# Four edits around the output stage and the last weight gradients of a one-core forward and backward kernel: a later first load of w2 rows, whole-piece weight transposes, log-dt turned as bf16, another PSUM pool for the last output tile

## The chip, the core and the metric

The kernel runs on one core of a Trainium2 chip. Its engines are TensorE (PE in the profile; PEld is its weight load), VectorE (DVE), ScalarE (ACT), GpSimd (POOL) and SyncE (SP). Each works through its own instruction stream in order; an instruction waits for the semaphores of what it depends on, and everything behind it on the same engine waits too. SP, ACT and POOL also issue DMAs, which move data between device memory and the on-chip memories (SBUF, and PSUM, into which PE writes). "SPq" marks a DMA instruction on SP; its time is the time SP is held by issuing it, not the transfer. The metric is the device time of one execution, in microseconds.

## The reference, cut to what matters

The kernel computes a block's output and the gradients of all its parameters. `x` is 2048 tokens by D = 576, F is 4608.

```python
xn = layernorm(x)
s = ssm(xn, A, B, C, log_dt, Dskip)               # a long convolution, dt = exp(log_dt)
g = silu(((silu(xn @ w1) * (xn @ w3)) @ w2))      # SwiGLU, then silu
out = x + s * g
_out, vjp = jax.vjp(f, x, A_re, A_im, B_re, B_im, C_re, C_im, log_dt, Dskip, w1, w3, w2)
return (_out, *vjp(grad_out))
```

Three results of the backward half matter here: the gradients of w1, w3 and w2 (out_10 to out_12); the gradient of the input, which needs the two hidden gradients times the transposed w1 and w3 (out_1); and the gradients of the recurrence's parameters, which need dt (out_2 to out_8).

## The kernel before, in words

Tokens are cut into 16 tiles of 128, F into 36 blocks of 128 and, for the backward half, into 18 groups of 256. The order on each engine comes from a scheduler that takes instructions by a due time (`self.at`); `issue_after(x)` puts an instruction behind x, `sp`, `gp` and `sc` chain the instructions of one queue, and the pools decide which buffer a tile gets and what must have let go of it.

**Forward.** A hidden stage computes both gate products and stores h in device memory as `H_dram`, while the convolution runs beside it. The output stage (`ffn_output`) multiplies h by w2: for each token tile i, `begin(i)` turns the tile's 4608 columns of h onto the partitions by one transposing DMA on SP (`hcA`, `hcB` and `hcC` in turn; the DMA is kept in `hc_loads[i]`), and `product` runs 72 matmuls (`po`) into one of three PSUM pools, psA, psB, psC, chosen by i % 3. `finish(i)` then reads `po` with one ACT and two DVE instructions (lines 1119, 1122, 1123), forms out_0 and the gradient that goes into the SwiGLU (`go_o`), and PE turns that (`turn_go`, line 1165).

**Backward.** `backward` opens a pool of three one-bank PSUM tiles (`ph`) and one of two (`pgw`) in the space that psA, psB and psC leave. For each of the 18 groups it needs the group's w2 turned (`w2T`): two rows of blocks are loaded as `w2r` (line 1618) and turned by SP (`phase6_load_w2`, through the helper line 1640, `nat_transpose`). Line 1708 forms the hidden gradient `ph`, line 1726 (DVE) the two products `gu_n` and `gg_n`, line 1731 stores them (`GU_dram`, `GG_dram`), line 1748 makes w2's gradient and line 1768 those of w1 and w3. Between them run the backward convolution (lines 816 to 862, 1267 to 1329) and, from group 4 on, the parameter sums (`param_step`: `qT`, `gz` and `pz` are loaded by SP, line 1372 on PE, lines 1377 and 1380 on DVE).

**The turned weights.** The input gradient (`phase6_inputs`, line 1818, `px`) takes 72 blocks: for each token tile the rows of `GG_dram` and `GU_dram` are turned into `acts`, and multiplied with the rows of w1 and w3 turned. 15 blocks of w1 and 11 of w3 have room of their own (`wA`) and are loaded over earlier groups. The other 46 go into buffers as the groups free them, by `load_piece`: six pieces of 7 blocks and two of 2. One piece (`h_n` tag, blocks 22 to 28 of w3) is loaded in the last group but one, three at the stage "h1" of the last group, then come the group's stores, the `acts` of two tiles, and the last four pieces. A piece is loaded by five transposing DMAs, one for each 128 (the last 64) of the 576 rows. `ready` counts the blocks with which both first token tiles begin.

**log-dt.** `phase5_open` loads the 576 values as five rows (`lg_b`) on POOL in the last group's stage "h3", ACT takes the exponential (line 1398, `er_b`, fp32), and `phase5_turn` turns the result on PE (line 1404) and copies it from PSUM on DVE (line 1405). Both tiles rotate through the three `gh6` buffers.

```python
with self.tc.issue_after(self.hc_loads[4].ins):       # backward, line 1520
    self.w2row_load(0)
for c in range(self.cfg.DT):                          # load_piece, line 1624
    self.load_wT_rows(wT[-1], c)
self.nat_transpose(w2T[:, fl], self.w2rows[gi % 2][:, fl])   # phase6_load_w2, line 1652
```

Of the kernel before, what the change touches and what calls it, by code (L numbers as in the profile page):

```python
# [10 lines left out]
ACT = mybir.ActivationFunctionType  # L11
ALU = mybir.AluOpType
AX = mybir.AxisListType
FP32 = mybir.dt.float32
BF16 = mybir.dt.bfloat16
I32 = mybir.dt.int32
I16 = mybir.dt.int16
P = 128
# [68 lines left out]
class K:  # L87
# [24 lines left out]
    def pool(self, **kw):  # L112
        return self.tc.tile_pool(reuse_waits="tile", **kw)
# [928 lines left out]
    def ffn_output(self, T0, TB):  # L1042
        nc, cfg = self.nc, self.cfg
        D, DT, L, LT, F, FT = cfg.D, cfg.DT, cfg.L, cfg.LT, cfg.F, cfg.FT
# [7 lines left out]
        with self.pool(name="o_gap", bufs=1) as gap, \  # L1052
# [38 lines left out]
            def begin(i):  # L1091
                self.at(T0 + TB * i)
                hc = (self.wtp, hp, hpc)[i % 3].tile([P, FT, P], BF16, name="hc" + "ABC"[i % 3], tag=("WT", "hcB", "hcC")[i % 3])
                for f0, f1, step in turns[i] if i < 3 else ((0, FT, None),):
                    with self.tc.issue_after(self.h_stores[step].ins) if step else nullcontext():
                        ld = self.nat_transpose(hc[:, f0:f1], self.H_dram[i][:, f0 * P:f1 * P])
                self.hc_loads.append(ld)
                x_t = ip3.tile([P, D], BF16, name="x_t")
                go_t = ip3.tile([P, D], BF16, name="go_t")
                s_t = ip4.tile([P, D], BF16, name="s_t4")  # L1100
                nc.gpsimd.dma_start(out=x_t[:], in_=self.tok("A_u", i))
                nc.gpsimd.dma_start(out=go_t[:], in_=self.tok("grad_out", i))
                nc.gpsimd.dma_start(out=s_t[:], in_=self.S_dram[:, i, :])
                return i, hc, x_t, go_t, s_t, (psA, psB, psC)[i % 3].tile([P, 2, 512], FP32, name="po")

            def product(st, f0, f1, after=None):
                hc, po_ = st[1], st[5]
# [7 lines left out]
            def finish(st):  # L1115
# [23 lines left out]
                if i < LT - 1:  # L1139
                    self.turn_go(i, pst.tile([P, DT, P], BF16, name="ptr"))  # L1140

            first = begin(0)
            self.at(self.gate_time(70) - 1)
            product(first, 0, F0, self.tails[69])
# [10 lines left out]
            for i in range(2, LT):  # L1155
                st = begin(i)
                product(st, 0, FT)
                finish(st)
# [224 lines left out]
    def phase5_open(self, pool):  # L1383
        nc, cfg = self.nc, self.cfg
        self.fp = pool
        self.NB = -(-cfg.D // P)
        NB = self.NB
        lr = pool.tile([NB, P], BF16, name="lg_b", tag="gh6")
        st = self.small.tile([P, 3 * NB + 3], FP32, name="sm_b")
        self.dtb = st[:, 0:2 * NB].rearrange("p (k j) -> p k j", k=2)  # L1390
        self.gl = st[:, 2 * NB:3 * NB]
        self.acc = st[:, 3 * NB:]
        nc.vector.memset(lr[:], 0.0)
        nc.vector.memset(self.gl, 0.0)
        for row, vec in self.block_rows(lr, self.aps["A_log_dt"]):
            nc.gpsimd.dma_start(out=row, in_=vec)  # L1396
        self.er = er = pool.tile([NB, P], FP32, name="er_b", tag="gh6")
        nc.scalar.activation(out=er[:], in_=lr[:], func=ACT.Exp)

    def phase5_turn(self):  # L1400
        nc, NB, er = self.nc, self.NB, self.er
        pt = self.ps_T.tile([P, 512], FP32, name="et_ps")
        with self.tc.issue_after(self.pe_last.ins):
            nc.tensor.transpose(pt[:, 0:NB], er[:], self.ident_f[0:NB, 0:NB])
        nc.vector.tensor_copy(out=self.dtb[:, 0], in_=pt[:, 0:NB])
        nc.vector.tensor_tensor(out=self.dtb[:, 1], in0=self.dtb[:, 0], in1=self.dtb[:, 0], op=ALU.mult)
        self.final = self.phase5_blocks()
        self.final_rows = None
# [86 lines left out]
    def backward(self, T0, TG, TQ, TC, TX, gctx, mats):  # L1495
        nc, cfg = self.nc, self.cfg
        D, L, LT, F, FT = cfg.D, cfg.L, cfg.LT, cfg.F, cfg.FT
# [7 lines left out]
        pool = self.pool  # L1505
        PS = bass.MemoryType.PSUM
        FA, GP = 14, 11
        with ExitStack() as out:
# [4 lines left out]
            elp = out.enter_context(pool(name="e_el", bufs=3))  # L1513
# [3 lines left out]
            self.w2rows = [rowp.tile([P, self.FG // P, cfg.DT * P], BF16, name=f"w2r{i}") for i in range(2)]  # L1517
            for w2r in self.w2rows:
                nc.gpsimd.memset(w2r[:, :, D:cfg.DT * P], 0.0)
            with self.tc.issue_after(self.hc_loads[4].ins):  # L1520
                self.w2row_load(0)
            ps_h = ffn.enter_context(pool(name="e_ps_h", bufs=3, space=PS, side="right"))
            ps_gw = ffn.enter_context(pool(name="e_ps_gw", bufs=2, space=PS, side="right"))
# [22 lines left out]
            wT = []  # L1546
            for ai, n in ((0, 15), (1, 11)):
                wT.append((ai, 0, n, wA.tile([P, n, D], BF16, name=f"wA{ai}")))
            self.params_open(S_all, ps)
            step = self.param_step  # L1550
            hs = {}
            for gi in range(NG):
                self.chain = gi >= GP
                lastg = gi == NG - 1
                nxt = self.phase6_load(gi + 1, T0 + TG * gi, TG, wp, inp) if not lastg else None
                prep = nxt[-1] if nxt else iter(())
                if lastg:
                    self.tail()
                self.at(T0 + TG * gi)
                hs[gi] = cur[1]  # L1560
                w2 = lambda g, fl: self.phase6_grad2(g, fl, hs[g], gwp, ps_gw)
                for stage in group if gi == 0 else self.phase6_group(gi, cur, elp, gwp, ps_h, ps_gw):
                    if stage == "h3" and self.chain and gi + 2 < NG:
                        self.w2Ts[gi + 2] = self.phase6_load_w2(gi + 2, wp)
                    if stage in ("h2", "h3", "out_11_0", "out_11_1", "out_11_2", "out_11_3", "out_10_0", "out_10_1"):
                        next(prep, None)
                    if stage in ("h1", "h3"):
                        if gi < NG - 1:
                            w2(gi, stage == "h3")
                        elif stage == "h3":  # L1570
                            self.phase5_open(elp)
                        if stage == "h3" and gi + 2 < NG:
                            self.phase6_load_h(gi + 2, T0 + TG * gi, inp)
                    if stage == "out_11" and gi == NG - 2:
                        self.load_piece(wT, inp, "h_n", 1, 22, 7)
                    if stage == "h1" and lastg:
                        self.load_piece(wT, inp, "gg_n", 0, 15, 7)
                        self.load_piece(wT, inp, "gu_n", 1, 15, 7)
                        self.load_piece(wT, wp, "w2T", 1, 13, 2)
                    if stage == "end" and 0 <= gi - GP < cfg.DT:  # L1580
                        for part in wT[0:2]:
                            self.load_wT_rows(part, gi - GP)
                    if stage == "stored":
                        c = gi - GP
                        if c in (1, 2, 3, 4):
                            step()
                        if lastg:
                            self.hold = []
                            self.phase5_turn()
                            acts = [self.load_acts(0)]  # L1590
                            for fl in range(2):
                                w2(gi, fl)
                                step()
                                self.phase5_step(self.half // 2)
                                self.phase5_step(self.half // 2)
                            acts.append(self.load_acts(1))
                            self.ready = sum(part[2] for part in wT)
                            self.load_piece(wT, wp, "w2T", 1, 11, 2)
                            self.load_piece(wT, inp, "h_n", 0, 22, 7)
                    elif stage in ("h1", "h3", "out_11", "out_10", "end") and gi >= GP and not (lastg and stage in ("out_10", "end")):  # L1600
                        step()
                        if lastg and stage == "out_11":
                            self.phase5_step(self.half // 2)
                            self.phase5_step(self.half // 2)
                cur = nxt
# [15 lines left out]
    def load_piece(self, wT, pool, tag, ai, f0, n):  # L1621
        t = pool.tile([P, n, self.cfg.D], BF16, name=f"wT{ai}_{f0}", tag=tag)
        wT.append((ai, f0, n, t))
        for c in range(self.cfg.DT):
            self.load_wT_rows(wT[-1], c)

    def load_wT_rows(self, part, c):
        ai, f0, n, t = part
# [19 lines left out]
    def phase6_load_w2(self, gi, wp):  # L1648
        nfl = self.FG // P
        w2T = wp.tile([P, nfl, self.cfg.DT, P], BF16, name="w2T")  # L1650
        for fl in range(nfl):
            self.nat_transpose(w2T[:, fl], self.w2rows[gi % 2][:, fl])
        if (gi + 1) * self.FG < self.cfg.F:
            self.w2row_load(gi + 1)
        return w2T
# [341 lines left out]
```

## Time and profile before

| | us |
|---|---|
| three runs | 1818.41, 1829.12, 1833.62 |
| their median | 1829.12 |
| the profiled execution | 1822.4 |
| its span, first to last instruction | 1820.6 |
| PE busy | 1664.9 (91%) |
| VectorE busy | 1358.7 (75%) |
| ScalarE busy | 911.6 (50%) |
| mean granted TensorE clock | 0.982 |

Busy time says how long an engine had work in hand. What an edit is worth is read from the waits: a line of the waits such as `A <- B: 9.9, 5, 3.0` says that A waited 9.9 us in total for B, in 5 waits of at most 3.0 us. In a timeline a row gives start, time, engine, line, operation, tiles and count, and in brackets the idle time before it with what ended it. "DMA share" is the busy share of the 16 DMA engines.

| stretch of the profiled execution, us | what runs | PE busy | DMA share |
|---|---|---|---|
| 605 to 635 | output stage, tiles 5 to 7 | 22.93 of 30 | 1.16 |
| 635 to 704 | output stage, tiles 7 to 13 | 66.84 of 69 | 0.86 |
| 724 to 745 | end of the last output tile, group 0 opens | 16.91 of 21 | 0.76 |
| 745 to 765 | convolution and group 0 | 12.32 of 20 | 0.11 |
| 1436 to 1456 | last group | 14.46 of 20 | 0.82 |
| 1475 to 1490 | first input-gradient tiles | 12.68 of 15 | 1.14 |
| 1490 to 1505 | the same, last pieces being turned | 14.73 of 15 | 0.86 |
| 1505 to 1522 | the same | 7.82 of 17 | 0.94 |
| 1540 to 1560 | token tile 2 of the input gradient | 13.36 of 20 | 1.15 |

### The profile page before, as it was taken

What the parts mean: (1) busy time and instruction counts of PE and PEld (TensorE: products, weight loads), DVE (VectorE), ACT (ScalarE), POOL (GpSimd) and SP (SyncE); (2) the same over time, 40 slices, a digit from 0 to 9 for tenths busy, and PEclk for the clock granted to TensorE, in tenths of its full rate; (3) what the DMA queues carried; (4) which work ended last, traced back from release to release, by engine and by line L of the source; (5) the groups of instructions that cost most, each with busy time, mean ns of one, the idle gap of its engine ahead of it and who ended that gap; (6) DMA issues with size and microseconds to landing.
All of it is one profiled execution on the core that took longest, in us unless ns stands there. A gap on an engine that the chain in (4) does not pass through costs nothing. (4 is left out here: it accounts for less than half of the span.)

```text
span 1820.6 us, 38755 instructions
## 1 busy us (share of the span) xinstructions
PE 1664.9 (91%) x15573; PEld 1232.7 (68%) x15637; DVE 1358.7 (75%) x2103; ACT 911.6 (50%) x1648; POOL 346.3 (19%) x565
## 2 busy tenths in 40 slices
PE   7789999999999899799999999999899896999997
PEld 3455555554546677678888888888688774777885
DVE  7778888795873455767977879569899945878675
ACT  6778888776862111765756666554345310001001
POOL 3112222123143110011111101111111233131032
PEclk9999999999999999899999999999999998999999
DMA  7889998879699985478665756689999999999992
GB/s 221 275 280 344 321 343 312 279 266 285 208 296 226 222 208 150 149 217 237 188 192 174 208 162 203 165 253 241 253 228 226 195 225 207 236 217 224 220 251 52
DMA packets 636506, 416.91 MB, mean 229 GB/s; under 512 B 425430, under 2 KB 576966, under 8 KB 631718
## 3 DMA queue, kind: packets, MB, share of 16 engines
q1 hardware_dynamic: 580644, 287.34, 63.6%
q0 software_dynamic: 31904, 106.81, 18.2%
q10 hardware_dynamic: 23778, 20.28, 4.1%
q8 instruction: 122, 2.00, 0.5%
q14 instruction: 58, 0.48, 0.1%
HBM read 135.60 MB, written 190.89 MB: 179 GB/s over the span
## 5 line engine op out<-in xcount | busy, mean ns | idle before, releaser
L1818 PEld LDWEIGHTS <-acts 128*128 128x128 bf16 x2304 | 226.0, 99 | 81.5 <-DMA acts<-GU_dram 9.2
L1768 PEld LDWEIGHTS <-xn_bf 128*128 128x128 bf16 x2304 | 224.8, 98 | 46.7 <-issue 20.2
L1818 PE MATMUL px<-wT,acts 128*128 128x288 bf16 x1472 | 193.3, 289 | 9.9 <-DMA wT<-in_B_w_dram 9.9
L1377 DVE TENSOR_TENSOR pr_q<-et_ps,pz 128x1024 f32<-128x1024 f32 x144 | 175.8, 1221 | 27.0 <-PE et_ps L1372 10.5
L1708 PE MATMUL ph<-w2T,goT 128*128 128x256 bf16 x1440 | 175.5, 275 | 6.1 <-ACT gh L1711 3.4
L1011 PEld LDWEIGHTS <-xnT 128*128 128x128 bf16 x1152 | 107.0, 98 | 108.8 <-issue 17.7
L1380 DVE TENSOR_REDUCE S_all<-pr_q 128x32 f32<-128x1024 f32 x144 | 175.2, 1217 | 3.1
L1708 PEld LDWEIGHTS <-goT 128*128 128x128 bf16 x1440 | 140.4, 99 | 25.4 <-issue 5.4
L1011 PE MATMUL pu<-wmB_w,xnT 128*128 128x512 bf16 x568 | 152.9, 379 | 0.5 <-issue 0.2
L1748 PE MATMUL pgw<-go_o,h_n 128*128 128x288 bf16 x1152 | 150.0, 288 | 3.4 <-DVE h_n L1686 2.7
L1011 PE MATMUL pg<-wmB_w,xnT 128*128 128x512 bf16 x526 | 143.6, 379 | 8.2 <-issue 5.6
L1768 PE MATMUL pgw<-gu_n,xn_bf 128*128 128x256 bf16 x1152 | 136.6, 274 | 12.2 <-ACT gw L1752 6.2
L1748 PEld LDWEIGHTS <-h_n 128*128 128x128 bf16 x1152 | 113.1, 99 | 32.4 <-DVE h_n L1686 3.0
L1768 PE MATMUL pgw<-gg_n,xn_bf 128*128 128x256 bf16 x1152 | 130.4, 272 | 2.4 <-ACT gw L1770 2.3
L1770 ACT CAST gw<-pgw 128x256 bf16<-128x256 f32 x144 | 52.2, 373 | 147.3 <-PE pgw L1768 147.2
L1025 ACT ACTIVATE s_t<-pg 128x512 bf16<-128x512 f32 x144 | 87.8, 610 | 73.6 <-PE pu L1019 42.8
L1818 PE MATMUL px<-wA,acts 128*128 128x288 bf16 x832 | 112.0, 291 | 11.7 <-DMA acts<-GU_dram 8.6
L1711 ACT CAST gh<-ph 128x512 bf16<-128x512 f32 x144 | 80.9, 597 | 63.7 <-PE ph L1708 63.1
L660 ACT ACTIVATE cs_k<-et_ps 128x512 bf16<-128x512 int16 x216 | 111.5, 633 | 0.1
L1039 POOL DMA_DIRECT2D G_dram<-g_t x72 | 52.2, 726 | 288.1 <-DVE g_t L1029 146.2
L1874 ACT ACTIVATE go<-gx 128x576 bf16<-128x576 f32 x16 | 10.9, 683 | 188.8 <-DVE gx L1857 105.3
L1030 ACT CAST u_t<-pu 128x512 bf16<-128x512 f32 x144 | 87.5, 608 | 7.6 <-PE pu L1011 7.5
(317 smaller groups left out, 3208.9 us busy)
## 6 DMA issues: line engine op xcount, KB each, us to landing
U_dram<-u_t POOLq DMA_DIRECT2D x72, 256.0 KB, 5.6
G_dram<-g_t POOLq DMA_DIRECT2D x72, 256.0 KB, 5.0
H_dram<-h_t SPq DMA_DIRECT2D x72, 256.0 KB, 3.9
Q_dram<-q_k SPq DMA_DIRECT2D x36, 512.0 KB, 4.5
h_n<-U_dram POOLq DMA_DIRECT2D x18, 1024.0 KB, 8.8
gg_n<-G_dram POOLq DMA_DIRECT2D x18, 1024.0 KB, 6.7
GU_dram<-gu_n SPq DMA_DIRECT2D x36, 512.0 KB, 5.0
GG_dram<-gg_n SPq DMA_DIRECT2D x36, 512.0 KB, 10.3
```

The costliest lines, as they stand in the source:

```text
L660: self.sin_last = nc.scalar.activation(out=CS[:, :, o:o + 256], in_=pt[:].bitcast(I16)[:, :, 0::2], func=ACT.Sin, scale=6.283184 / 2 ** 16)
L1011: ins = nc.tensor.matmul(pt[:], lhsT=xnT[:, c, ts], rhs=wm[w][:, c, :], start=(q == 0 and c == 0), stop=(q == 1 and c == nfull - 1))
L1025: nc.scalar.activation(out=s_t[:, :, q, :], in_=pgv, func=ACT.Silu)
L1030: nc.scalar.copy(out=u_t[:, :, q, :], in_=puv)
L1039: self.u_stores[step] = nc.gpsimd.dma_start(out=dst[fb * ng:(fb + 1) * ng, :, i0:i0 + NT, :].rearrange("g p t f -> p g (t f)"), in_=src[:] ...
L1377: nc.vector.tensor_tensor(out=pr[:].rearrange("p r k e -> p r (k e)"), in0=T[h][:].rearrange("p k z d a -> p (k z d a)")[:, None].to_broad ...
L1380: nc.vector.tensor_reduce(out=self.S_all[:, :, d0:d0 + 4], in_=pr[:].rearrange("p r k (d a) -> p (r k) d a", d=4), op=ALU.add, axis=AX.X)
L1708: self.pe_last = nc.tensor.matmul(ph[j][:, k, :].rearrange("p (a f) -> p a f", f=P), lhsT=lw, rhs=rh, start=(n == 0), stop=(n == nfull))
L1711: self.sc(lambda: nc.scalar.copy(out=gh[:, j], in_=ph[j][:]))
L1748: self.pe_last = nc.tensor.matmul(pgw[pi_][:, 0:pw], lhsT=hn[:, tt, fl * P:(fl + 1) * P], rhs=go_o[:, tt, po:po + pw], start=(tt == 0), st ...
L1768: self.pe_last = nc.tensor.matmul(pw_[:, 0:FG], lhsT=self.xn_bf[:, tt, c * P:(c + 1) * P], rhs=nat[:, tt, :], start=(tt == 0), stop=(tt == ...
L1818: self.pe_last = nc.tensor.matmul(px[pi_][:, 0:pw], lhsT=acts[i][:, ai, fi, :], rhs=w[:, po:po + pw], start=(n == 0), stop=(n == len(steps ...
```

## The change

It makes four edits.

1. The last output tile takes PSUM pool psC, like the tile before it, instead of psA.
2. The first w2 rows (`w2row_load(0)`) are put behind the output stage's eighth tile load instead of the fifth, and group 0's turned w2 behind the fourteenth.
3. A weight piece is turned by one DMA of 576 source rows instead of five of 128 or 64. `wA` is still loaded in rows.
4. log-dt is loaded when the backward half opens, into a tile of its own (`lg_r`), on POOL's chained queue. PE turns it as bf16, and ACT takes the exponential from PSUM straight into `dtb`; the DVE copy goes.

```diff
@@ ffn_output, begin @@
-                return i, hc, x_t, go_t, s_t, (psA, psB, psC)[i % 3].tile([P, 2, 512], FP32, name="po")
+                return i, hc, x_t, go_t, s_t, (psA, psB, psC)[i % 3 if i < LT - 1 else 2].tile([P, 2, 512], FP32, name="po")
@@ phase5_open @@
-        lr = pool.tile([NB, P], BF16, name="lg_b", tag="gh6")
+        self.lr = lr = self.small.tile([NB, P], BF16, name="lg_r")
...
         for row, vec in self.block_rows(lr, self.aps["A_log_dt"]):
-            nc.gpsimd.dma_start(out=row, in_=vec)
-        self.er = er = pool.tile([NB, P], FP32, name="er_b", tag="gh6")
-        nc.scalar.activation(out=er[:], in_=lr[:], func=ACT.Exp)
+            self.gp(lambda: nc.gpsimd.dma_start(out=row, in_=vec))
@@ phase5_turn @@
-        pt = self.ps_T.tile([P, 512], FP32, name="et_ps")
+        pt = self.ps_T.tile([P, 512], FP32, name="et_ps")[:].bitcast(BF16)[:, 0:NB]
         with self.tc.issue_after(self.pe_last.ins):
-            nc.tensor.transpose(pt[:, 0:NB], er[:], self.ident_f[0:NB, 0:NB])
-        nc.vector.tensor_copy(out=self.dtb[:, 0], in_=pt[:, 0:NB])
+            nc.tensor.transpose(pt, self.lr[:], self.ident_bf[0:NB, 0:NB])
+        nc.scalar.activation(out=self.dtb[:, 0], in_=pt, func=ACT.Exp)
@@ backward @@
-            with self.tc.issue_after(self.hc_loads[4].ins):
+            with self.tc.issue_after(self.hc_loads[7].ins):
                 self.w2row_load(0)
...
             self.params_open(S_all, ps)
+            self.phase5_open(elp)
...
-                        elif stage == "h3":
-                            self.phase5_open(elp)
@@ load_piece @@
-        for c in range(self.cfg.DT):
-            self.load_wT_rows(wT[-1], c)
+        self.nat_transpose(t[:], self.aps[("B_w1", "B_w3")[ai]][:, f0 * P:(f0 + n) * P])
@@ phase6_load_w2 @@
         for fl in range(nfl):
-            self.nat_transpose(w2T[:, fl], self.w2rows[gi % 2][:, fl])
+            with self.tc.issue_after(self.hc_loads[13].ins) if gi == 0 else nullcontext():
+                self.nat_transpose(w2T[:, fl], self.w2rows[gi % 2][:, fl])
```

In the order of instructions that the scheduler makes of it, three things move beyond the edited lines. On SP, the four w2T transposes of groups 0 and 1 go from between the loads of tiles 4 and 6 to between those of tiles 13 and 14, and four of the six w2r loads that stood among them with them. On PE, 21 `ph` matmuls of group 0 stand ahead of the last output tile's first matmul. On DVE and ACT, the convolution's work after the last output tile is ordered anew: the `gk_st` evictions of lines 1322 and 1325 for the first two blocks stand ahead of group 0's Silu (line 1678) on ACT, and on DVE one fold (lines 1267, 1268) and a further part of the convolution's products (lines 856 to 862) stand ahead of group 0's lines 1685 and 1686.

More of the change, by code (lines that the diff above doesn't have):

```diff
@@ L1395, in phase5_open @@
         for row, vec in self.block_rows(lr, self.aps["A_log_dt"]):
-            nc.gpsimd.dma_start(out=row, in_=vec)
-        self.er = er = pool.tile([NB, P], FP32, name="er_b", tag="gh6")
-        nc.scalar.activation(out=er[:], in_=lr[:], func=ACT.Exp)
+            self.gp(lambda: nc.gpsimd.dma_start(out=row, in_=vec))
     def phase5_turn(self):
-        nc, NB, er = self.nc, self.NB, self.er
-        pt = self.ps_T.tile([P, 512], FP32, name="et_ps")
+        nc, NB = self.nc, self.NB
+        pt = self.ps_T.tile([P, 512], FP32, name="et_ps")[:].bitcast(BF16)[:, 0:NB]
         with self.tc.issue_after(self.pe_last.ins):
-            nc.tensor.transpose(pt[:, 0:NB], er[:], self.ident_f[0:NB, 0:NB])
-        nc.vector.tensor_copy(out=self.dtb[:, 0], in_=pt[:, 0:NB])
+            nc.tensor.transpose(pt, self.lr[:], self.ident_bf[0:NB, 0:NB])
+        nc.scalar.activation(out=self.dtb[:, 0], in_=pt, func=ACT.Exp)
         nc.vector.tensor_tensor(out=self.dtb[:, 1], in0=self.dtb[:, 0], in1=self.dtb[:, 0], op=ALU.mult)
```

## The prediction

> **What bounds the kernel now.** I read the chain of work that ended last, then PE's waits by stretch, then SP's timeline where a wait ends on a DMA.
>
> ```profile
> PE 14%; SPq 3%; DMA 2%; DVE 1%; issue 0%; ACT 0%; POOL 0%; ACTq 0%; DVEq 0%
> ```
>
> The chain is followed back through the last fifth of the span only, and PE has 14 of those 20 points: PE sets the end, and the rest is SP and its transfers. So an edit is worth what it takes from PE's waits. Those from the last group on (1400 to 1821), in us, times, longest:
>
> ```profile
> PE px L1818 <- DMA wT<-in_B_w_dram: 9.9, 5, 3.0
> PE px L1818 <- DMA acts<-GU_dram: 8.6, 2, 7.8
> PE et_ps L1372 <- DMA gz<-gK_dram: 7.1, 3, 3.6
> PE et_ps L1404 <- ACT er_b L1398: 4.4, 1, 4.4
> PE px L1818 <- DMA acts<-GG_dram: 3.1, 1, 3.1
> ```
>
> SP there, as start, time held, instruction:
>
> ```profile
> 1435.69 20.32 SPq L1640 DMA_TRANSPOSE wT<-in_B_w_dram  x15
> ...
> 1460.16 1.03 SPq L1731 DMA_DIRECT2D GU_dram<-gu_n  x2
> 1461.29 3.57 SPq L1731 DMA_DIRECT2D GG_dram<-gg_n  x2
> 1467.50 6.24 SPq L1640 DMA_TRANSPOSE acts<-GG_dram  x1
> ...
> 1490.46 28.88 SPq L1640 DMA_TRANSPOSE wT<-in_B_w_dram  x20
> 1519.44 4.91 SPq L1640 DMA_TRANSPOSE acts<-GG_dram  x1
> ```
>
> SP is held 20.3 us by three pieces, ahead of the stores that the first `acts` need, and 28.9 us by the last four, for which PE waits. Held time against size, for the helper's groups (min/median/max, ns):
>
> ```profile
> L1640 SPq DMA_TRANSPOSE wT<-in_B_w_dram x40: 1232/1284/3658, 1415.3 to 1518.1; - x40
> L1640 SPq DMA_TRANSPOSE acts<-GG_dram x16: 4769/5602/11166, 1467.5 to 1768.5; - x16
> ```
>
> A fifth of a piece (at most 7 blocks of 128x128) takes as long as a quarter of a 36-block `acts`. The output stage, SP and then PE:
>
> ```profile
> 596.56 4.48 SPq L1640 DMA_TRANSPOSE w2T<-w2r  x3
> 601.13 6.75 SPq L1640 DMA_TRANSPOSE hcC<-H_dram  x1
> 608.55 1.22 SPq L1640 DMA_TRANSPOSE w2T<-w2r  x1
> ...
> 612.52 5.74 SPq L1640 DMA_TRANSPOSE hcA<-H_dram  x1
> ```
> ```profile
> 611.17 5.55 PE L1111 MATMUL po<-w2a,hcC 128*128 128x288 bf16 x32 [4.37 <-DMA hcC<-H_dram]
> 624.83 5.55 PE L1111 MATMUL po<-w2a,hcA 128*128 128x288 bf16 x32 [2.70 <-DMA hcA<-H_dram]
> 635.62 4.08 PE L1111 MATMUL po<-w2a,hcB 128*128 128x288 bf16 x32
> ```
>
> PE waits for two tile loads that stood behind w2T on SP; after a wait the same 32 matmuls take 5.55 instead of 4.08 us. Last, where group 0 opens (724 to 800):
>
> ```profile
> PE et_ps L827 <- DVE ZZ L1309: 5.7, 2, 3.9
> PE ph L1708 <- DVE e L1123: 2.7, 1, 2.7
> PE pgw L1748 <- DVE h_n L1686: 2.7, 1, 2.7
> ```
>
> **Edit 2, the w2 rows: -9.3.** From one first matmul to the next, tiles 5 and 6 take 15.33 and 13.49 us (606.8, 622.13, 635.62) against a steady pitch of 9.77: 5.56 + 3.72 = 9.3 over. Without w2r and w2T before it, SP reaches hcC of tile 5 at about 594 instead of 601.1. PE began it 10.0 us after SP did (611.17 - 601.13), so it is ready by 604, where PE wants it at 606.8. The same reckoning puts hcA of tile 6 at 614.5, wanted at 616.6. That cover is 2 us; where it fails, the edit gains 5 instead. The four w2T and four w2r (some 7.5 us of SP) then push the load of tile 14 from 684.9 to at most 689.5, ready by 699 where PE wants it at 704: nothing, while those 5 us last. Group 0 needs w2T at 700 or later; its four turns would end by then too.
>
> **Edit 1, psC, and the new order around it: +3.5.** Tile 15 must wait for line 1123 of tile 14, by the timeline some 3.5 us after tile 14's last matmul. In front of it PE now has 21 `ph` matmuls, 21 x 0.114 = 2.4 us, so about 1.2 us are a true wait and the rest is work done early. What goes is the 2.7 that `ph` waited for e after tile 15. Queued behind the waiting matmul are all of tile 15 and `turn_go`. On DVE two folds and some five products (together 4.8 us by the spacing of their rows, 0.67 and 0.37) now stand ahead of lines 1685 and 1686, and on ACT two blocks' gk_st evictions ahead of the Silu, with its table loads and derivative 10.4 us (1.28 + 3.90, twice). `h_n`, for which line 1748 already waited 2.7, comes later by up to 4.8 + 1.2. Against that the convolution runs ahead by as much, and its waits for ZZ (5.7) may shrink. No row shows this order; ends are -4 (most of the 5.7 gone, h_n no later) and +9 (h_n 6 later, and 3 of tile 15 not made up). I take +3.5: nearer to h_n's wait plus the 1.2, less part of ZZ's. In POOL's queue four small loads of log-dt (2.05 us together by their rows at line 1396) come between the parts of `gg_n`, where POOL stood idle 4.67: nothing; unhidden it would cost 2.
>
> **Edits 3 and 4, the last group and the first input-gradient tiles: -18.** Price of a piece: 31.5 blocks by the `acts` rows of 36, 4.77 to 6.24 us, is 4.2 to 5.5; I take 4.5, near their minimum, since five smaller ones already reach theirs. A two-block piece (9 blocks) 1.3, the wT median. The first set is then 1.4 + 2 x 4.5 = 10.4 instead of 20.3. SP's stores go from 1460 to about 1449, bounded by when DVE has made gu_n, and the first `acts` are issued near 1459 and not 1467.5; px can start when PE is ready. That was 1473.4; without the 4.4 for er_b DVE binds: of its work behind, only 2.4 is saved (DVE stood idle 1450.2 to 1452.65 and is full after), so about 1471, against 1476.45 before. From there PE has 98 matmuls before the last pieces, twice (196 x 0.1225 = 24 us with the convolution sums among them): 1496. The second set starts after the two `acts` pairs, at about 1476; at 1.4 + 3 x 4.5 = 15 it is held to 1491 and landed by 1499 (transposes of wT land at most 4.9 us after issue; I add 2 for the larger ones). PE needs the last piece no earlier than 1502: five waits, 9.9 us, and the slow matmuls after them go. Tile 0 ends at about 1502.1 and tile 1 at 1507.3, but a new wait follows: `acts` of tile 2 needs tile 0's buffer, so it is issued at 1502.2, used 9 us later, 1511.2, a wait of 3.9. Tile 2 began at 1529.0: 1511.2 - 1529.0 = -17.8. The 7.75 us for its GU stay, since SP issues it behind a `gz` that waits for PE. PE works from the end of tile 1 on as before.
>
> With x for a piece, landing is about 1476 + 5x: nothing changes to x = 5.5, at 6.5 the gain is 14, at 9.3 nothing is left of it, and at 10.4 the whole change breaks even. Range -20 (the new wait half hidden) to -14.
>
> The piece loaded in the last group but one saves SP 5 of its 9.76 us at 1415; SP then waits for PE: nothing, and no price without that. Edit 4 moves the table load of Exp (1.28 + 0.31) to after line 1404, at the 13th matmul of line 1748; ACT has its next cast there some 3 us later. Two DVE instructions (0.26 us) go. The gz waits (7.1) hang on order and stay, within 4 either way.
>
> Sum: -9.3 + 3.5 - 18 = -23.8. The profiled execution took 1822.4, 6.7 below the median of 1829.1: 1798.6 of its own, 1805.3 against the median.
>
> **One rule against the price of a piece.** The `acts` row says 1.18 MB in 4.77 to 6.24 us of SP's time, and the forecast scales that. The Trainium skill (DMA: Bandwidth & Descriptors, Latency and other measured facts) gives transposing DMAs 261 GB/s where the middle dimension isn't contiguous, which makes an estimated 4.0 us of a piece's 1.03 MB. By the same page (Bandwidth, its measured table) 1 MB takes 6.15 us, for a plain load from GpSimd; by that the sum would be near -20.5, and five small transfers would have been paid for by data, not by count.
>
> **Rivals.**
>
> *Data sets the piece, not count (10%).* The first set took 20.32 us for 15 transfers, 1.35 each, and its data don't shrink. Five by 1.27 to 1.3 are 6.35 to 6.5: C gives 14, the whole 20: 1809. For it: DMA share 1.14 at 1475 to 1490. Against it: the same 1.28 for a w2T of 5 blocks as for a wT of 7.
>
> *The opening of group 0 costs 9 or more (12%).* Line 1748 already waits for h_n; if DVE runs its new order without recovery, gain about 15: 1814.
>
> *The waits of tiles 5 and 6 come from crowded DMA engines (6%).* The share is 1.16 there against 0.86 later. Then w2T isn't the cause, A is nothing: 1815. Against it: SP's row order puts both loads right behind w2T.
>
> *The other side: one transfer of 576 rows is much slower than five (10%).* No row shows a turn of more than 128 rows. If such a piece is held twice 6.5, 13 us, the last lands at 1476 + 65 = 1541, tile 2 starts 19 us later than before and not 18 sooner: -9.3 + 3.5 + 19 = +13, 1842. It decides from 10.4 us a piece on. For it: maxima of 11.2 us in the `acts` row. Against it: its median of 5.6.
>
> That the change does less than it says I give nothing: the instruction order has 8 wT transposes instead of 40.
>
> **The numbers.** The forecast has 62%. The three runs of before lie 15 us apart, so I can't place the median better than some 5 us. Its own range adds the bounds: 1796 to 1817. With the two rivals at 1809 to 1815 and part of the slow one the range is 1792 to 1821. A measurement here tells 1% (18.3 us) from no change: below 1810.8 lie some four fifths of the forecast, half of the data rival and a third of the next, 0.50 + 0.05 + 0.04, and a few points of the rest: 0.62. Above 1847.4 lies the slow rival from 14.1 us a piece on, half of its chance, and two points for group 0's new order going wrong past every gain: 0.07. The rest, 0.31, is within 1%.
>
> **What would show it.** Right: eight wT transposes on SP, six of 4.2 to 5.5 us; no wait for wT and none for er_b; tiles 5 and 6 at a pitch of 9.8; px starting some 5 us sooner; a new wait of about 4 for acts<-GG_dram at tile 2; a longer wait for h_n. Wrong: pieces over 6.5 us, waits for the loads of tiles 14 or 15, or PE idle at 745 to 765 by more than 9 us over before.

## The result, and the profile after

| | before | changed |
|---|---|---|
| median, us | 1836.43 (16 runs, 1818.41 to 1848.12) | 1813.45 (16 runs, 1801.66 to 1826.32) |
| ratio, 95% interval | | 0.9894 (0.9864 to 0.9925) |
| the profiled execution's span | 1820.6 | 1819.7 |

The change makes the kernel 1.06% faster; of 1829.1 us that is 19.4, between 13.7 and 24.9. The forecast was 23.8. Ratios here and below leave out executions over 1.5% above the fastest of their kernel: three of the sixteen before (the medians of all lie 23.0 apart), and three of six with edit 1 undone, its profiled one among them, which therefore counts in no mean. The two profiled executions differ by 0.9 us only, so their spans would have told a reader that nothing happened. What tells the parts apart is the time between marks that PE passes in each profile: the first matmul of an output tile (counted from 0, as `hc_loads` is; the expectations below call the marks of tiles 4 and 14 tiles 3 and 13), the first w2-gradient matmul of a group (line 1748 before, 1745 after), the first and the last matmul of the input gradient.

| stretch, us | before | changed | |
|---|---|---|---|
| start to output tile 4 | 596.9 | 597.1 | +0.2 |
| output tile 4 to 14 | 107.4 | 98.5 | -8.9 |
| output tile 14 to group 4 | 213.7 | 219.3 | +5.6 |
| group 4 to 13 | 355.6 | 355.6 | 0 |
| group 13 to 17 | 166.1 | 173.9 | +7.8 |
| group 17 to token tile 2 of the input gradient | 89.3 | 75.6 | -13.7 |
| token tile 2 to the last px matmul | 280.0 | 288.1 | +8.1 |

The stretches that the forecast spoke of sum to -17.0. The two to which it gave nothing, group 13 to 17 (where edit 3 changes one weight piece) and the tail, were 15.9 longer in this execution.

PE's waits from the last group on, in the changed kernel (1400 to 1821; us in all, times, longest):

```profile
PE px L1815 <- DMA acts<-GU_dram: 10.9, 2, 7.3
PE et_ps L1372 <- DMA gz<-gK_dram: 8.9, 2, 6.4
PE px L1815 <- DMA acts<-GG_dram: 6.3, 2, 4.2
PE et_ps L1402 <- DVE pr_q L1377: 1.5, 1, 1.5
```

The waits for wT (9.9) and for er_b (4.4) are gone. The one for GG at tile 2 (4.2) is new, as forecast. GU is waited for at tile 2 as before (7.3, before 7.8), and the wait for it at tile 0 has grown. SP there:

```profile
1439.77 10.22 SPq L1636 DMA_TRANSPOSE wT<-in_B_w_dram  x3
...
1455.80 1.02 SPq L1728 DMA_DIRECT2D GU_dram<-gu_n  x2
...
1464.07 6.72 SPq L1636 DMA_TRANSPOSE acts<-GG_dram  x1
1470.88 5.85 SPq L1636 DMA_TRANSPOSE acts<-GU_dram  x1
1476.83 7.75 SPq L1636 DMA_TRANSPOSE acts<-GG_dram  x1
1484.63 6.75 SPq L1636 DMA_TRANSPOSE acts<-GU_dram  x1
1491.43 15.88 SPq L1636 DMA_TRANSPOSE wT<-in_B_w_dram  x4
1510.75 4.82 SPq L1636 DMA_TRANSPOSE acts<-GG_dram  x1
```

Three pieces hold SP 10.2 us and not 20.3, four 15.9 and not 28.9. All eight pieces (six of 7 blocks, two of 2), held time of one, min/median/max in ns:

```profile
L1636 SPq DMA_TRANSPOSE wT<-in_B_w_dram x8: 1357/4357/7741, 1420.0 to 1502.1; - x8
```

And where PE's row of the first input-gradient matmuls shows what it waited for:

```profile
1475.44 3.85 PE L1815 MATMUL px<-wA,acts 128*128 128x288 bf16 x30 [2.14 <-DMA acts<-GG_dram]
1482.94 2.87 PE L1815 MATMUL px<-wA,acts 128*128 128x288 bf16 x22 [3.66 <-DMA acts<-GU_dram]
...
1498.79 17.07 PE L1815 MATMUL px<-wT,acts 128*128 128x288 bf16 x138
1520.03 5.22 PE L1815 MATMUL px<-wA,acts 128*128 128x288 bf16 x21 [4.16 <-DMA acts<-GG_dram]
```

The 138 matmuls on wT run through at 0.124 us each. But GU of tile 0 comes 3.66 us late, where before it came 0.87 late.

The output stage, SP and then PE:

```profile
595.79 7.79 SPq L1636 DMA_TRANSPOSE hcC<-H_dram  x1
...
604.85 6.13 SPq L1636 DMA_TRANSPOSE hcA<-H_dram  x1
```
```profile
607.81 4.09 PE L1111 MATMUL po<-w2a,hcC 128*128 128x288 bf16 x32 [0.47 <-DMA hcC<-H_dram]
617.14 4.08 PE L1111 MATMUL po<-w2a,hcA 128*128 128x288 bf16 x32
```

The load of tile 5 starts 5.3 us sooner and that of tile 6 7.7; 4.37 and 2.70 of waiting become 0.47 and nothing, and the 32 matmuls take 4.1 us at once. Where group 0 opens (715 to 790):

```profile
PE et_ps L827 <- DVE ZZ L1309: 8.7, 2, 6.1
PE pgw L1745 <- DVE h_n L1683: 4.9, 1, 4.9
```

The wait for e after the last tile (2.7 in `ph`; 0.7 is left, at line 816) is gone; those for ZZ and h_n have grown from 5.7 and 2.7 to 8.7 and 4.9.

### The profile page after: what moved, and what is told of

Same layout as the page of the kernel before. It is cut to its first block, busy times and chain, and to the rows that moved or that the text cites. A ratio compares the mean times of both kernels' runs of the same rounds, so it can differ in the third digit from the quotient of the medians.

```text
span 1819.7 us, 38713 instructions
## 1 busy us (share of the span) xinstructions
PE 1668.7 (92%) x15573; PEld 1235.1 (68%) x15637; DVE 1359.7 (75%) x2102; ACT 912.0 (50%) x1648; POOL 346.5 (19%) x565
## 5 line engine op out<-in xcount | busy, mean ns | idle before, releaser
L1030 ACT CAST u_t<-pu 128x512 bf16<-128x512 f32 x144 | 87.5, 608 | 7.6 <-PE pu L1011 7.4
```

What stands on the lines that cost most here:

```text
L1030: nc.scalar.copy(out=u_t[:, :, q, :], in_=puv)
```

## The experiments

Each ratio is to the kernel before, run beside it, with its 95% interval. Since the times spread by some 15 us either way, the verdicts rest on the stretches first and on the ratios second.

**Edit 1 undone.**

```diff
-(psA, psB, psC)[i % 3 if i < LT - 1 else 2]
+(psA, psB, psC)[i % 3]
```

> The changed kernel with edit 1 undone: the last output tile takes PSUM pool psA again. Read from the first matmul of output tile 13 to the first w2-gradient matmul of group 4: 213.7 us before, 219.3 after, so this stretch lost 5.6. Theory (the new order around psC costs what the stretch lost: PE runs into waits for ZZ and h_n): the stretch is 212 to 215, and the time is 4 to 6 us under the changed kernel's, ratio to before about 0.986. Rival (the stretch lost to the w2 rows that now stand late on SP, or to chance): it stays at 218 to 220 and the ratio at 0.989.

Ratio 0.9856 (0.9801 to 0.9911), from three executions; over all six the ratio of the medians is 0.9918. Output tile 14 to group 4 took 214.9, and the waits are near those of before:

```profile
PE et_ps L827 <- DVE ZZ L1309: 5.8, 2, 3.9
PE ph L1705 <- DVE e L1123: 3.5, 1, 3.5
PE pgw L1745 <- DVE h_n L1683: 3.2, 1, 3.2
```

So the new order, and the stretch's loss with it, come from the pool. The other profiles say the same, and the two groups do not overlap: psC 216.4 to 219.6 (five, mean 218.0) with a wait for h_n of 4.9 in every one; psA 213.0 to 215.2 (eight, mean 214.2) with 2.7 to 2.9 for h_n and 5.7 to 5.8 for ZZ. Edit 1 costs 3.8 us there. That the kernel without it gains as much as a whole isn't shown by the ratios: the intervals overlap.

**Edit 2 undone.**

```diff
-            with self.tc.issue_after(self.hc_loads[7].ins):
+            with self.tc.issue_after(self.hc_loads[4].ins):
...
-            with self.tc.issue_after(self.hc_loads[13].ins) if gi == 0 else nullcontext():
-                self.nat_transpose(w2T[:, fl], self.w2rows[gi % 2][:, fl])
+            self.nat_transpose(w2T[:, fl], self.w2rows[gi % 2][:, fl])
```

> The changed kernel with edit 2 undone: first w2 rows behind the fifth tile load, w2T without its wait. Read from the first matmul of tile 3 to that of tile 13: 107.4 us before, 98.5 after. Theory (SP's order made tiles 5 and 6 wait): 106 to 109, with waits for hcC and hcA of 2 to 5 us at tiles 5 and 6, ratio about 0.994. Rival (crowded DMA engines made them wait, and the changed kernel's profile was lucky): 98 to 101, no such waits, ratio as that of the changed kernel.

Ratio 0.9971 (0.9933 to 1.0009). Tile 4 to 14 took 104.3, less than expected, with the waits of the output stage (540 to 724) back, though shorter at tile 6 (hcA) than the expected 2 to 5:

```profile
PE po L1111 <- DMA hcC<-H_dram: 7.3, 2, 4.1
...
PE po L1111 <- DMA hcA<-H_dram: 1.1, 1, 1.1
```

The three kernels with early w2 rows took 104.3 to 107.4 (mean 106.14), ten with late ones 97.9 to 98.5 nine times and once 101.7 (mean 98.38). Edit 2 is worth 7.8 us. (The ratio lost 14 us with it, more than this stretch; where the rest went isn't shown.) Crowded DMA engines are not the reason: from 605 to 635 their share is 1.16 before, with the waits, and 1.18 in the changed kernel, without, and over the whole stretch they are busier where the waits are gone. Tile 4 to 14 of before, then of the changed kernel; the last three columns are granted clock, DMA share and GB/s:

```profile
596.90:704.30 107.40, 97.89 (x773) 74.30 (x771) 55.40 (x80) 14.21 (x31) 16.12 (x30) 0.97 0.96 207
```
```profile
597.10:695.60 98.50, 94.98 (x773) 72.96 (x771) 56.49 (x82) 14.21 (x31) 16.66 (x31) 1.00 1.14 218
```

**Edit 3 undone.**

```diff
-        self.nat_transpose(t[:], self.aps[("B_w1", "B_w3")[ai]][:, f0 * P:(f0 + n) * P])
+        for c in range(self.cfg.DT):
+            self.load_wT_rows(wT[-1], c)
```

> The changed kernel with edit 3 undone: each weight piece by five transposes again. Read from the first w2-gradient matmul of group 17 to the first matmul of token tile 2 of the input gradient: 89.3 us before, 75.6 after. Theory (the number of transposes holds SP, and PE waits for pieces and acts): 85 to 89, waits for wT of 8 to 11 in five or so, the last four pieces hold SP 27 to 30; ratio about 0.996. Rival (most of the gain is edit 4's, which lets the stage begin sooner): 76 to 81, waits for wT under 4, ratio about 0.991.

Ratio 1.0017 (0.9975 to 1.0060), where 0.996 was expected. The stretch took 87.5. The first three pieces held SP 20.61 us and the last four 27.53, and PE waited for wT 6.7 in five (a little under the expected 8):

```profile
PE px L1816 <- DMA wT<-in_B_w_dram: 6.7, 5, 2.5
```

By the ratio all of the change's gain goes with this edit, 22 us; by the stretch 12. The next run tells the two apart.

**Edit 3 alone**, on the kernel before.

> The kernel before with edit 3 alone: weight pieces by one transpose each. From group 17's first w2-gradient matmul to token tile 2: 89.3 us before, 75.6 with all edits, 87.5 with all but this one. Theory (this edit alone is worth 12 to 14 us there, and nothing elsewhere): 75 to 79, the wait for er_b still 4 to 5, no wait for wT, ratio 0.992 to 0.994. Rival (the times, by which undoing it cost 22 us, are right, and it gains outside this stretch too): the same stretch, but ratio 0.987 to 0.989, and another stretch that is shorter.

Ratio 0.9931 (0.9891 to 0.9971), stretch 74.1: by time as the theory says, by stretch a little better; the wait for wT is 0.9, not nothing. Ten profiles with whole pieces took 72.6 to 75.7 from group 17 to tile 2 (mean 74.2; with edit 1 undone it was 78.6), the two with five rows for every piece 89.3 and 87.5: edit 3 is worth 14.2 us.

**The last four pieces in rows, the first four whole.**

```diff
-        self.nat_transpose(t[:], self.aps[("B_w1", "B_w3")[ai]][:, f0 * P:(f0 + n) * P])
+        if len(wT) < 7:
+            self.nat_transpose(t[:], self.aps[("B_w1", "B_w3")[ai]][:, f0 * P:(f0 + n) * P])
+        else:
+            for c in range(self.cfg.DT):
+                self.load_wT_rows(wT[-1], c)
```

> The changed kernel with the last four pieces alone turned by five transposes each, the four before them whole. Theory (what counts is when the last pieces land): the input gradient's first matmul comes 28 to 32 us after group 17's first w2-gradient matmul, as in the changed kernel (31.0), but from there to tile 2 it takes 52 to 56 instead of 44.6, with waits for wT of 8 us or more. Rival (what counts is the earlier start by the first pieces; the last then have time): from the first matmul to tile 2 44 to 48.

Ratio 0.9961 (0.9924 to 0.9998). The first px matmul came 31.6 us after group 17, as with whole pieces; from there to tile 2 it took 51.2, just under the range, with 7.1 of waiting for wT where 8 was expected. The stretch is 82.8, so the last four pieces carry 8.6 of the 14.2 (82.8 - 74.2) and the first ones the other 5.6, by which the stores and acts come sooner.

**Edit 4 undone.**

```diff
-            self.phase5_open(elp)          # when the backward half opens
+            elif stage == "h3":            # in the last group
+                self.phase5_open(elp)
...
-            nc.tensor.transpose(pt, self.lr[:], self.ident_bf[0:NB, 0:NB])
-        nc.scalar.activation(out=self.dtb[:, 0], in_=pt, func=ACT.Exp)
+            nc.tensor.transpose(pt[:, 0:NB], er[:], self.ident_f[0:NB, 0:NB])
+        nc.vector.tensor_copy(out=self.dtb[:, 0], in_=pt[:, 0:NB])
```

> The changed kernel with edit 4 undone: log-dt loaded in the last group, exponential before the turn. Same stretch as for the five rows (89.3 before, 75.6 after). Theory (DVE binds there, so of er_b's 4.4 us only about 2.4 are worth something, and part of that is covered by the wait for the first acts): 76 to 79, the wait of PE for er_b is back with 3 to 5 us, ratio 0.989 to 0.991. Rival 1 (the whole wait counts): 79.5 to 81, ratio 0.992. Rival 2 (the first acts end the wait anyway): 75 to 76.

Ratio 0.9918 (0.9878 to 0.9958). The wait at line 1404 is back (put down to another load, which came last), and the stretch is 74.0: the second rival holds, edit 4 is worth nothing there. Where it goes can be seen in px's rows of this run:

```profile
PE et_ps L1404 <- DMA pz<-PZ_dram: 5.3, 1, 5.3
```
```profile
1473.53 6.54 PE L1818 MATMUL px<-wA,acts 128*128 128x288 bf16 x52
...
1492.81 17.07 PE L1818 MATMUL px<-wT,acts 128*128 128x288 bf16 x138
1513.59 4.63 PE L1818 MATMUL px<-wA,acts 128*128 128x288 bf16 x26 [3.71 <-DMA acts<-GG_dram]
```

All 52 matmuls on wA run without a break: px starts later, and GU is there. In the three kernels with whole pieces and the old log-dt px starts 32.9 to 33.9 us after group 17 and needs 40.1 to 41.2 more to tile 2; in the seven with the new one it starts at 28.8 to 31.5 and needs 43.8 to 44.7. Less the wait for GG that precedes px in five of them, PE was ready at 28.8 to 28.9 in all seven. The 4 to 5 us won are spent mostly on waits for GG and GU. GU itself also landed sooner in this run than in the changed kernel, 34.4 us after group 17 against 38.5; whether the new log-dt has a part in that isn't shown.

**Edits 2 and 3 alone**, on the kernel before.

> The kernel before with edits 2 and 3 alone. Theory (they carry the whole gain, edit 1 costs 4 to 5, edit 4 is worth at most 2): tile 3 to 13 98 to 99, tile 13 to group 4 213 to 216, group 17 to tile 2 75 to 79, sum of the three 386 to 394 against 410.4 before and 393.4 after; ratio 0.986 to 0.989. Rival (edit 4 is needed for part of it): the last of the three at 79 to 82.

Ratio 0.9888 (0.9836 to 0.9940). The stretches took 97.9, 215.2 and 73.4, together 386.5 where the changed kernel took 393.4. The two edits give all that the change gives, and edits 1 and 4 aren't needed for any of it.

**GU of tile 2 ahead of the parameter loads**, with edit 1 undone.

```diff
+                self.load_acts(i + 2, (1,), acts[i])
                 if i == 0:
                     self.param_flush()
-                self.load_acts(i + 2, (1,), acts[i])
```

> The changed kernel with psA again (edit 1 undone) and one step more: the second half of tile 2's acts is issued on SP ahead of the two groups of parameter loads that stood before it. From tile 2's first matmul to tile 3's: 31.0 in the changed kernel, 28.1 with psA, of it a wait for GU of 7.3. Theory (SP's order makes PE wait): 20 to 24, no wait for GU at tile 2, and 4 to 7 us less in the whole than with psA alone. Rival (the parameter loads come later and PE waits for gz in its place): 26 to 31, with a wait of line 1372 for gz of 4 us or more, and no gain.

Ratio 0.9907 (0.9867 to 0.9946). Token tile 2 to tile 3 took 23.3, as the theory says, and the wait for GU there is gone. But from tile 3 to the end it took 263.2, more than any profile up to then (248.1 to 260.8). The 4 to 7 us that the theory gave the whole are not shown.

**wA out of the groups where the parameters are summed.** Group 13 to 17 spreads from 160.0 to 181.0 us in ten profiles. In the changed kernel one row of wA (17.0 us) held SP for most of the following time, in which two rows are merged:

```profile
1308.44 18.76 SPq L1636 DMA_TRANSPOSE wA<-in_B_w_dram  x2
1327.30 2.77 SPq L1636 DMA_TRANSPOSE qT<-Q_dram  x1
```

Four kernels, all with edit 1 undone: the ten rows five groups sooner; two whole transposes at the ends of groups 11 and 12; the two whole ones from group 8 on; and the last with GU ahead of the parameter loads too.

```diff
-                    if stage == "end" and 0 <= gi - GP < cfg.DT:
-                        for part in wT[0:2]:
-                            self.load_wT_rows(part, gi - GP)
+                    if stage == "end" and 0 <= gi - GP < 2:        # or gi - GP + 3
+                        ai, f0, n, t = wT[gi - GP]
+                        self.nat_transpose(t[:], self.aps[("B_w1", "B_w3")[ai]][:, f0 * P:(f0 + n) * P])
```

> The changed kernel with psA again, and the ten row transposes of wA issued five groups sooner, so that SP has them behind it before the parameter loads begin. Group 13 to group 17, by their first w2-gradient matmuls, took between 159.9 and 181.0 us in ten profiles so far, with waits of line 1372 for gz of 2 to 20 us that go with it; no edit of the change touches that stretch. Theory (wA's transposes hold SP up to 23 us among the parameter loads, by chance, and PE waits for gz): 157 to 162, waits for gz under 4, ratio 0.980 to 0.985. Rival (the DMA queue is full there whatever stands in it, and qT or w2T is held in wA's place): 160 to 181 as before, ratio as with psA alone (0.986).

> The changed kernel with psA again, and wA by two transposes of 576 rows (15 and 11 blocks, at the ends of groups 11 and 12) instead of ten over five groups. By the whole pieces of 7 blocks (4.4 us, 0.62 a block) SP would be held 9.3 and 6.8 us. Theory of the count: 8 to 11 and 6 to 8 us held, and group 13 to 17 in 157 to 163 us, since eight row transposes leave it. Rival (a transfer of this size is held far longer): over 15 us for the larger, and the loss shows between groups 11 and 13, where the kernel before takes 74.4 us: 80 or more.

> The changed kernel with psA again, and wA by two whole transposes, issued in groups 8 and 9 or as soon as its room is free. Theory: as for the early rows (group 13 to 17 157 to 162, waits for gz under 4), with less of SP's time; ratio 0.980 to 0.985. Rival: SP waits there for wA's room with other loads behind it, groups 9 to 12 (by their first w2-gradient matmuls 108.6 us before) grow by 5 us or more and the time gains nothing over psA alone.

> The same with the second half of tile 2's acts ahead of the parameter loads too. Theory: that step is worth 4 to 7 us between tile 2's and tile 3's first matmul (23.2 us with it, 28.1 without) and keeps most of it: ratio 0.977 to 0.983. Rival (it is given back between tile 3 and the end): tile 2 to the last px matmul 285 to 292 as in five of the profiles so far, and a ratio no better than the run without it.

| | ratio (95%) | group 4 to 13 | of it 11 to 13 | 13 to 17 | tile 2 to the end |
|---|---|---|---|---|---|
| rows early | 0.9925 (0.9887 to 0.9963) | 378.2 | 96.3 | 156.8 | 293.8 |
| whole | 0.9902 (0.9867 to 0.9938) | 368.6 | 87.3 | 156.8 | 304.3 |
| whole, early | 0.9924 (0.9882 to 0.9965) | 368.2 | 85.0 | 156.8 | 285.8 |
| that and GU first | 0.9929 (0.9892 to 0.9967) | 368.1 | 84.8 | 156.8 | 295.5 |
| changed kernel | 0.9894 (0.9864 to 0.9925) | 355.6 | 74.4 | 173.9 | 288.1 |

The first theory is right in its place: without wA group 13 to 17 takes 156.8 four times, and PE waits for gz there 0.7 us in one of the four and not at all in the others (12.1 in the changed kernel). But the wait moves to where wA now stands: of the 17 us won, 12.5 to 22.6 are lost from group 4 to 13. In the run with whole transposes, between groups 11 and 13 (1195 to 1290):

```profile
PE et_ps L1372 <- DMA gz<-gK_dram: 11.9, 1, 11.9
```

There the larger transpose held SP 10.99 us and the smaller 6.52, as the count says, but the next parameter load stands behind the first. With the early whole ones the rival is right: group 9 to 12 takes 121.1 us against 108.6 before, and the transposes held SP 8.75 and 9.46 us, with GU first 9.06 and 13.70. With GU first token tile 2 to 3 took 24.6, and the rest gave it back, as that run's rival says. The ratios of 0.977 to 0.985 that the theories expected were missed by all four, and none is faster than the changed kernel. In three of them the time from tile 2 to the end exceeds every earlier profile (275.7 to 291.6); why stays open.

## Why the prediction was right

Right in sign, in the likeliest case and in size: 19.4 us measured of 23.8, with the median in the range. (Its own bounds add up to 1796 to 1819, not 1817; in its rivals, A is edit 2 and C edits 3 and 4.) By its own terms, measured as means over the profiles with and without the edit, which come to -18.2 together:

- **Edit 2, -9.3: measured -7.8**, between the 9.3 and the 5 that it gave for a cover that fails. SP reached tile 5's load at 595.8 (forecast about 594) and tile 6's at 604.85. The cover of 2 us was as thin as it said: the one profile of 101.7 lost it. The pitch of tiles 5 and 6 became 9.3 and 9.8.
- **Edit 1, +3.5: measured +3.8.** The wait for e after tile 15 went and h_n came later, as stated. But its wait grew by 2.2 and not by up to 6, tile 15 waited 0.2 and not 1.2, and ZZ, from which some was to be won back, grew by 3.0. That the sum fits so well is in part luck.
- **Edits 3 and 4, -18: measured -14.2.** The price of a piece was right: 4.36 us by the median against 4.5, and 15.9 for the last four against 15. Only the piece in the last group but one was held longer, 7.74, where nothing waits for it. By the count of bytes SP lets 1.03 MB go in 4.36 us, 237 GB/s; from issue to landing a piece took 8.4 to 8.9 us where the trace has it. The 261 GB/s for transposing DMAs in the Trainium skill (DMA: Bandwidth & Descriptors, Latency and other measured facts) comes near the held time; its 6.15 us for a plain load of 1 MB (Bandwidth) does not. The start of the stores (forecast 9 us after group 17, 11.4 measured) was close. That of px (31.3 forecast, 31.0 measured) was so by luck: PE was ready at 28.9, 4.8 sooner than before and not 2.4, and then waited 2.1 for GG.

The step that failed is "From there PE has 98 matmuls before the last pieces, twice": it let PE run from px's start to the last pieces without a wait, and so counted edit 4's 2.4 us as gained. From px's start to tile 2 it allowed 40.2 us; the changed kernel took 44.6. GU of tile 0 was issued at 1470.9 and used at 1482.9, and an earlier start of px only waits longer for it. The forecast gave no time to the second half of the first acts.

A second size was off, and did no harm. The last four pieces were to be issued about 36 us after group 17, behind two `acts` pairs that hold SP 17 us; the pairs held it 27 (23 before), and the pieces came at 47.0. The last landed 66.1 us after group 17, where the forecast had PE need it at 62.3; but PE, itself late by the wait for GU, did not wait for it. The cover was used up: in six of the eleven profiles with every piece whole PE waited for wT, for up to 1.5 us. That the waits for wT go came true with less room than the forecast said.

- **The rest, 0:** not borne out by these two profiles alone, with +7.8 in group 13 to 17 and +8.1 from tile 2 to the end. But group 13 to 17 varies between kernels whose code there is the same (171.8 with the last four pieces in rows, 181.0 with GU first), with the waits for gz.

The rivals: the piece that its data sets (6.4 us) fell to the 4.36; the slow transfer of 576 rows fell to it as well; the crowded DMA engines fell to the share that stayed as high when the waits went; group 0's opening at 9 or more fell to 3.8. The chance of 62% for more than 1% came true narrowly: 1.06%, and the interval reaches from 0.75% to 1.36%.

A version that beats the changed kernel beyond doubt was not found. Edit 1 undone has the lowest ratio (0.9856) and wins in the one stretch it touches, but the ratio rests on three executions.

## What to carry to other kernels

Where one queue issues in order, count what each DMA holds it: five transposes of a fifth cost SP half as much again as one of the whole (6.4 us against 4.36), and all that stands behind pays. Before a removed wait at the head of a stage is counted as gained, ask when the next transfer in the chain arrives; edit 4 removed 4.4 us of waiting and gained none. Compare two profiles by stretches between fixed marks: where the times spread by 1%, a difference of two spans says less than one stretch that never moves.

## What the runs showed of the hardware that was not expected

- Where no load on SP sets the pace, an execution repeats itself closely: group 4 to 13 took 355.4 to 355.8 us in the first ten profiles. Group 13 to 17, where PE waits for gz, took 160.0 to 181.0, though its code differs by one weight piece and the log-dt load at most. That the spread of the times comes from such places is suggested by this, not shown: each kernel has one profile.
- How long SP is held by a transposing DMA depends on where it stands. In the ten kernels that load wA in rows in groups 11 to 15, a transpose of 128 rows and 15 blocks held SP 2.1 to 23.0 us, and the one of 11 blocks right behind it 1.3 to 2.6; with the rows early it was 1.5 to 11.4 and 1.4 to 6.9. The piece in the last group but one held SP 7.6 to 7.8 in all twelve profiles where it is whole, the other whole pieces of its size 4.0 to 6.2. The held time is thus not the price of the transfer alone; what SP waits for is not in these traces.
- A transpose of 576 rows costs SP 0.62 us a block of 128 x 576 at 7 blocks (4.36), and 0.73 at 15 (10.99 in the run with whole transposes at groups 11 and 12); one of 128 rows and 7 blocks 1.28 us, 0.18 a block of 128 x 128, where the whole piece pays 0.14 (4.36 over 31.5).
